# Attention, expert attention and gated mixing on one core: the first batch issued in a written order, its loads reordered, five warming products fewer

## The chip, the core and the metric

The kernel runs on one core of a Trainium2 chip. The core has a matrix engine (PE, with its weight loads shown apart as PEld), a vector engine (DVE), an activation engine (ACT), a general engine (POOL) and a queue engine (SP), which issues nearly all DMAs here; 16 DMA engines move the data. The metric is the device time of one launch in microseconds, lower is better. Three timed runs of the kernel before gave 791.86, 794.79 and 794.84 us; their median, 794.79, is the time to compare with.

## The reference

Three stages in float32 over 8 batches of 576 tokens, each feeding the next:

```python
def _attn_ref(q, k, v, p):            # 8 batches, 8 heads, 576 tokens, 64 wide; p: 32 packed queries
    p_packed = sm_attn(p, k, v)       # softmax(p k^T / 8) v
    return sm_attn(q, p_packed, p_packed)

def _moe_ref(x, w_gate, wq, wk, wv, wo):   # 4 experts of causal attention, 2 of 4 kept per token
    logits = x @ w_gate                    # top 2, softmax over the two
    for e in range(4):
        q, k, v = x @ wq[e], x @ wk[e], x @ wv[e]
        out += weight(e) * (softmax(causal(q @ k.T / 8)) @ v) @ wo[e]

def _moe2_ref(x, mu_k, mu_r, w_k, w_v, w_r):
    xk = mu_k * x + (1 - mu_k) * x_prev    # x_prev: the token before
    xr = mu_r * x + (1 - mu_r) * x_prev
    v = relu(xk @ w_k) ** 2 @ w_v
    return sigmoid(xr @ w_r) * v
```

The weights `w_k`, `w_v` and `w_r` are float64 and are decoded on the chip.

## The kernel before

The work of the first two stages is cut into generators ("steps"): `front` (the first stage of a batch, for each of two groups `g` of four heads), `values`, `project`, `soft`, `turn` and `pair_out` (the second stage), and `fold`, which decodes `w_k` and `w_r` piece by piece and multiplies each by `wo`. Each `yield` of a step has a planned time from a table (`FRONT_T`, `G1_T`, `VAL_T`, `FOLD_0` and the others, in units of which a batch has 20). The program sorts all pieces by these times, issues them in that order, and a scheduler then orders the instructions of each engine by priority and by its own estimate of time. After the last batch come the `r` products, the `k` products and the `v` products of the third stage.

In the code, with the line numbers of the profile: the warming products (16 products of 128x128 on zeros, L168) come first on PE. `front` for one group is: scores `s1` of the packed queries, 8 products 32x288 (`eight`, L220); their maximum `mx` (L268) and `nb` (L270) on DVE; the exponential `a1` on ACT (L273); five transposes on PE (L280) and their copy `aT` on ACT (L205); the product with `v` (L289, 20 pieces); the scaled `pp` on DVE (L296), its transpose (L301) and the copy `ppT` (ACT, L205); the scores `s2` of the 576 tokens (L220 on `qT`); on DVE two transposes `st` (L308), the maximum `m` (L311), the subtraction (L313); the exponential on ACT (L316); the product with the packed input weights `wa` (L220) that is split into `PWh` (ACT, L319) and `PWl` (DVE, L320); the sums `s` (L323), `r` (L327, L328), the multiplication (L329), the transpose `a2` (L332), and its split into `A2h` (ACT, L205) and `A2l` (DVE, L335). The scores `s1`, the transposes, `s2` and the `wa` products share two buffers of PSUM (`big`), `aT` has one buffer.

`values` (L357) and `project` (L412) then take `A2h` and `A2l` of both groups. `project` ends in the casts `qs` and `ks` on ACT (L424, L430), the rest `l` and `kl` on DVE (L425, L431), and four small DMAs that move half a tile (L433, L434); after them the first score products of the second stage can run (L472). One chunk of `decode` is five DVE instructions (`dce` L625, `dcx` L628, `dce` L631, `dcu` L634, `wc` L655), one on ACT (`dcq` L645) and several on POOL; the folding products are L709.

The first loads stand on the SP queue in the order `p k` of both groups, `v q` of group 0, `wo`, two chunks `raw` of `w_k`, `v q` of group 1, the two halves of `wa`; then those of batch 1. For the first batch the small subtractions and multiplications (L313, L329) are on DVE, for the others on POOL. `decode` of the first chunks is held behind instructions of group 0 by `first` and `behind`.

Of the kernel before, what the change touches and what calls it, by code (L numbers as in the profile page):

```python
# [9 lines left out]
F32 = mybir.dt.float32  # L10
# [9 lines left out]
EPS = 1e-9  # L20
# [3 lines left out]
FRONT_T = [-29.98, -26.81, -23.33, -16.88, -17.51, -14.04, -12.67, -12.1, -8.35]  # L24
G1_T = [1.16, 2.59, 3.23, 1.72, 1.63, 8.19, 3.77, 1.61, 3.2]
VAL_T = [-3.35, 0.36, -1.9, 0.35, 0.62]
PROJ_T = [-2.04, -1.82, 1.38, 2.56]
# [4 lines left out]
FOLD_0 = [-21.99, -18.2, -16.87, -12.45, -10.56, -6.17, -3.87, -1.05, -0.52, 1.63, 3.63, 7.17, 8.98]  # L32
FOLD_T = [5.65, 105.86]
WA_AT = -29.61
PR0, WARM = (1000, 946, 1043, 1073, 1037, 1000, 940, 980, 907), 16
WR_AT = 7.41
R_LOAD, R_RUN = ([15.69, 16.11], [22.66, 28.61])
W_AT = [4.54, 4.19]
K_AT = [(0, -1.0, 0)] + [(0, 0.0, j) for j in range(4)] + [(1, -1.0, 0)] + [(1, 0.0, j) for j in range(5)]
E_TURN = "VAAAA"  # L40
E_DIAG = "AAAAV"
E_TURN2 = "AAAAA"
E_DIAG2 = "AAAVA"
E_WH, E_SQ, E_B, E_G, E_CXL = "P", "A", "V", "V", "A"
E_AT, E_VG, E_CB, E_PT, E_PPT, E_CX = "A", "A", "A", "V", "A", "V"
E_Z = "P"
E_DT, E_WL = "P", "P"
PR = {'front': 0, 'values': -100, 'project': 0, 'soft': 0, 'turn': 0, 'out': 236, 'fold': 0, 'k': 46, 'gates': 0}
# [7 lines left out]
def kernel(  # L56
# [83 lines left out]
    if True:  # L140
# [52 lines left out]
        def load_wa():  # L193
            for c in range(0, NG * NH, NH):
                nc.sync.dma_start(wa[:, c : c + NH, :], w_in[:, c : c + NH, :])

# [3 lines left out]
        def pool_copy(o, x):  # L200
            nc.gpsimd.tensor_scalar(o, x, 1.0, 0.0, op0=ALU.mult, op1=ALU.add)

        def evac(eng, o, x):
            if eng == "A":
                return nc.scalar.copy(o, x)  # L205
            if eng == "V":
                return nc.vector.tensor_copy(o, x)
            pool_copy(o, x)
# [4 lines left out]
        def eight(lhs, rhs, n):  # L213
# [3 lines left out]
            for j in range(NH):  # L217
                for hf in range(2):
                    r = slice(64 * hf, 64 * hf + 64)
                    nc.tensor.matmul(  # L220
# [4 lines left out]
                    )  # L225
            return halves(ps)[:, :, :n]

        def load(b, gs):

            for g in gs:  # L230
                pT = pTs[(b * NG + g) % 2]
                nc.sync.dma_start(pT, p[b, g].rearrange("d j n -> d (j n)"))
                kT = ld.tile([P, NH, SH], F32, tag="kT", name=nm("kT"))
                nc.sync.dma_start(kT, k[b, g])
                loaded[b, g] = [pT, kT]
            for g in gs:
                if b == 0 and g == 1:
                    first["won"] = dv.tile([P, NDT, 2 * P], F32, tag="wc", name=nm("won"), bufs=1)
                    nc.sync.dma_start(first["won"], wo.rearrange("(c p) n -> p c n", p=P))
                    first["raw"] = [fetch_raw(w_k, c * P, 0) for c in range(2)]  # L240
                vn = vns[(b * NG + g) % 2]
                nc.sync.dma_start(
                    vn[:, : NT - 1, :], v[b, g, : (NT - 1) * P].rearrange("(c p) x -> p c x", p=P)
                )
                nc.sync.dma_start(vn[TAIL:, NT - 1, :], v[b, g, (NT - 1) * P :])
                qT = ld.tile([P, NH, SH], F32, tag="qT", name=nm("qT"))
                nc.sync.dma_start(qT, q[b, g])
                loaded[b, g] += [vn, qT]

        def mark(b, g, eng, x, ins):  # L250

            if b == 0 and g == 0:
                for turn in {"V": [(0,), (1,), (2, 3)], "A": [(0, 1), (2, 3)]}[eng][x]:
                    first[eng, turn] = ins.ins

        def front(b, g):
# [847 lines left out]
```

## Time and profile before

| what | value |
|---|---|
| timed runs, median | 794.79 us (791.86 to 794.84) |
| profiled execution, whole | 789.45 us |
| profiled execution, first to last instruction | 787.7 us |
| PE busy | 751.6 us, 95% of the span |
| DVE busy | 477.4 us, 61% |
| ACT, POOL busy | 448.7 us, 384.5 us |

The profile comes from one execution. Its stretches differ: the opening (to about 46 us) in which the first batch's `front` has nothing before it to hide behind, the batches (to about 385 us), and the third stage. Shares over the whole span say little on the opening, so the rows below are stretches of it. The granted clock of PE has two levels here, 1.00 (2.4 GHz) and 0.50 (1.2 GHz).

### The profile page before, as it was taken

The numbers are of one execution on the slowest core, as the hardware profiler recorded it, in microseconds if no ns is written. First come the engines' busy times: TensorE is split into PE (matmuls) and PEld (weight loads), VectorE is DVE, ScalarE is ACT, GpSimd is POOL, SyncE is SP. The second block draws the span as 40 slices with busy tenths as digits, with TensorE's granted clock in tenths as the row PEclk, the third lists the DMA queues.
The fourth block names the chain that finished last, engine by engine and source line by source line (L and its number), as shares of the span: only waits on it lengthen the run. The fifth ranks groups of instructions, "written<-read, shape, count | busy, mean of one in ns | idle before, by whom it ended". The sixth has DMA issues, their size and how long they took to land.

```text
span 787.7 us, 15356 instructions
## 1 busy us (share of the span) xinstructions
PE 751.6 (95%) x5504; PEld 617.7 (78%) x5504; DVE 477.4 (61%) x1174; ACT 448.7 (57%) x1029; POOL 384.5 (49%) x484
## 2 busy tenths in 40 slices
PE   6789989999999999998999999999999999999998
PEld 4476968869697887877678888888888888888886
DVE  4979896979868668677767978787581111111111
ACT  2357677678767768786633532422967755555400
POOL 7358776764777635253601533631267443344610
PEclk9599999999999999999999999999999999999999
DMA  9856473655637353315459785867889565555511
GB/s 320 302 151 194 139 226 104 190 151 177 207 105 222 97 166 91 83 43 170 150 201 309 299 296 185 279 196 244 309 286 344 159 187 154 171 177 171 156 67 54
DMA packets 92396, 148.35 MB, mean 188 GB/s; under 512 B 9376, under 2 KB 64160, under 8 KB 90016
## 3 DMA queue, kind: packets, MB, share of 16 engines
q1 hardware_dynamic: 92176, 147.36, 58.7%
q8 instruction: 44, 0.72, 0.4%
q14 instruction: 32, 0.26, 0.1%
q10 hardware_dynamic: 144, 0.00, 0.0%
HBM read 87.04 MB, written 50.33 MB: 174 GB/s over the span
## 4 chain that ended last, share of the span: by engine, by line
PE 74%; DVE 11%; DMA 5%; POOL 4%; ACT 3%; issue 2%; SPq 0%; POOLq 0%; DVEq 0%; ACTq 0%
PE one L929 25%; PE big L888 8%; PE one L888 8%; PE one L557 5%; PE big L412 4%; PE one L868 4%; PE big L868 4%; DMA ms<-ms 4%; PE one L709 3%; PE one L357 3%; PE one L515 2%; PE one L472 2%; DVE ms L490 2%; ACT ms L494 1%; PE big L220 1%
## 5 line engine op out<-in xcount | busy, mean ns | idle before, releaser
L934 DVE TENSOR_TENSOR ring<-one,ring 128x512 f32<-128x512 f32 x36 | 24.9, 692 | 168.3 <-PE one L929 158.8
L929 PE MATMUL one<-wvh,yh 128*128 128x512 f32 x288 | 112.0, 389 | 0.0
L929 PE MATMUL one<-wvl,yh 128*128 128x512 f32 x288 | 112.0, 389 | 0.0
L929 PE MATMUL one<-wvh,yl 128*128 128x512 f32 x288 | 112.0, 389 | 0.0
L494 ACT ACTIVATE ms<-ms,nb 128x192 f32<-128x192 f32 (+3 forms) x128 | 78.4, 616 | 21.3 <-DVE nb L490 21.2
L211 POOL TENSOR_TENSOR yl<-yvh,yh 128x1024 fp32r<-128x1024 f32 (+1 forms) x24 | 49.1, 2060 | 44.7 <-ACT yh L914 24.6
L205 ACT COPY tb<-one 64x128 f32<-64x128 f32 (+5 forms) x208 | 61.4, 362 | 11.3 <-PE one L522 11.2
L640 POOL TENSOR_TENSOR dcx<-dcx,dcu 128x256 f32<-128x256 f32 x40 | 30.7, 768 | 66.1 <-DVE dcu L634 53.5
L929 PEld LDWEIGHTS one<-wvh,yh 128*128 128x128 f32 x288 | 54.1, 188 | 11.3
L929 PEld LDWEIGHTS one<-wvl,yh 128*128 128x128 f32 x288 | 54.1, 188 | 11.3
L929 PEld LDWEIGHTS one<-wvh,yl 128*128 128x128 f32 x288 | 54.1, 188 | 11.1
L211 POOL TENSOR_TENSOR yl<-yvl,yh 128x1024 fp32r<-128x1024 f32 x16 | 38.2, 2396 | 41.0 <-ACT yh L914 19.7
L515 PE MATMUL one<-ident,ms 128*128 128x128 f32 x320 | 53.1, 281 | 3.1 <-ACT ms L494 3.0
L557 PE MATMUL one<-tb,vg 128*64 128x320 f32 (+4 forms) x448 | 53.6, 362 | 0.6 <-DVE nb L490 0.4
L490 DVE CUSTOM_DVE_ANT_0 ms<-one,mstrip 128x192 f32<-128x192 f32 (+2 forms) x96 | 43.5, 481 | 15.9 <-PE one L472 15.2
L557 PEld LDWEIGHTS one<-tb,vg 128*64 128x64 f32 x448 | 33.3, 136 | 18.3 <-issue 1.7
L515 PEld LDWEIGHTS one<-ident,ms 128*128 128x128 f32 x320 | 36.2, 141 | 13.5 <-ACT ms L494 8.3
L211 POOL TENSOR_TENSOR dt<-cb 128x192 f32<-128x192 f32 (+1 forms) x48 | 31.4, 684 | 30.9 <-DVE cb L575 24.2
L1051 ACT ACTIVATE ring<-ring 128x1024 f32<-128x1024 f32 x18 | 19.0, 1059 | 34.9 <-DMA ring<-rscr 34.9
L472 PE MATMUL one<-ks,qs 128*128 128x192 f32 (+3 forms) x128 | 36.6, 300 | 0.4 <-ACT vg L205 0.3
L522 PE MATMUL one<-ident,ms 128*128 128x128 f32 x96 | 27.4, 287 | 9.3 <-DMA ms<-ms 8.7
L661 POOL TENSOR_TENSOR wl<-wc,wh 128x256 fp32r<-128x256 f32 x48 | 34.9, 751 | 0.3
(208 smaller groups left out, 2071.1 us busy)
## 6 DMA issues: line engine op xcount, KB each, us to landing
yscr<-y SPq DMA_DIRECT2D x48, 384.0 KB, 3.5
dl<-dscr SPq DMA_DIRECT2D x40, 256.0 KB, 5.8
yvh<-yscr SPq DMA_DIRECT2D x10, 1024.0 KB, 5.9
kT<-in_k_dram SPq DMA_DIRECT2D x16, 576.0 KB, 4.2
qT<-in_q_dram SPq DMA_DIRECT2D x16, 576.0 KB, 5.7
rscr<-rr SPq DMA_DIRECT2D x12, 768.0 KB, 4.4
ring<-rscr SPq DMA_DIRECT2D x36, 256.0 KB, 2.9
out_dram<-ring SPq DMA_DIRECT2D x36, 256.0 KB, 3.2
```

The costliest lines, as they stand in the source:

```text
L205: return nc.scalar.copy(o, x)
L211: nc.gpsimd.tensor_tensor(o, x, y, op=op)
L412: nc.tensor.matmul(ps[:, 512 * hf : 512 * hf + SH], ww[:, g, :], xx[:, g, :], start=i == 0, stop=i == 3 * NG - 1,)
L472: nc.tensor.matmul(ps[:, po : po + kn], qs[:, qo : qo + P], keys[:, ko : ko + kn], start=x == 0, stop=x == 1,)
L490: nc.vector.tensor_tensor_reduce(halves(mv) if last else mv, sv, halves(mk) if last else mk, op0=ALU.add, op1=ALU.min, scale=-SC, scalar=3 ...
L494: nc.scalar.activation(to, mv, AF.Exp, bias=nb[:n], scale=-1.0, accum_out=bat["sums"][:n, i, e : e + 1],)
L515: nc.tensor.transpose(ps[:, at + j * P : at + (j + 1) * P], ms[:, j * P : (j + 1) * P], ident)
L557: nc.tensor.matmul(av[64 * ee : 64 * ee + 64, qo - lo : hi - lo], vg[:, j, HD * (2 * ep + ee) : HD * (2 * ep + ee + 1)], tslice(tabs[ee], ...
L661: nc.gpsimd.tensor_sub(l, x, f32(h))
L868: nc.tensor.matmul(po, dx[:, NS * t + s, t0 : t0 + P], wpart("r", s, wx, t), start=n == 0, stop=n == 3 * KT - 1,)
L888: nc.tensor.matmul(po.rearrange("p (b n) -> p b n", b=2), wpart("k0" if f < 4 else "k1", s, wx, t)[:, f % 4 * P : f % 4 * P + P], dx[:, :, ...
L929: nc.tensor.matmul(ps, a[:, f, P * t : P * t + P], wres["v"][b][:, f, :], start=n == 0, stop=n == 3 * NFT - 1,)
```

## The change

For batch 0 every product of PE and the instructions of DVE and ACT that lie on the way of `front` are issued in the order in which the steps are given (`seq`, which ties each to the one before it on its engine). That order comes from new tables of step times, one for each group (`OPEN_T0`, `OPEN_T1`); batch 0 no longer uses `FRONT_T`. The decoding of the first piece is tied behind later instructions than before (`TIES_V`, `TIES_A`). The loads of the first batch are listed by name in `LOADS`. The warming products go from 16 to 11, and `fill` puts seven small products (128x64) on zeros behind some steps of the first batch. The other tables of times and priorities have new values, and the copy of the last diagonal block of a head (`E_DIAG[4]`, 64x64) goes from DVE to ACT in batches 0 to 3. What is computed stays the same.

```diff
-FRONT_T = [-29.98, -26.81, -23.33, -16.88, -17.51, -14.04, -12.67, -12.1, -8.35]
+FRONT_T = [-30.06, -26.81, -23.33, -16.88, -17.51, -14.67, -12.67, -12.1, -8.35]
+OPEN_T0 = [-30.95, -26.9, -23.4, -18.5, -18.46, -16.91, -15.8, -12.55, -12.53]
+OPEN_T1 = [-29.74, -25.62, -23.14, -17.97, -18.04, -18.19, -15.74, -12.38, -12.36]
...
+LOADS = 'k0 k1 v0 v1 q1 q0 wo wa r r'
+TIES_V, TIES_A = [5, 3, 5, 5], [5, 4, 5, 5]
+FILL = [[0, 4, 0, 0, 1, 0], [0, 2, 0, 0, 0, 0]]
+SEQ = 'VTA'
-PR0, WARM = (1000, 946, 1043, 1073, 1037, 1000, 940, 980, 907), 16
+PR0, WARM = (1050, 946, 1080, 1073, 1037, 896, 869, 980, 1107), 11
...
-E_DIAG = "AAAAV"
+E_DIAG = 'AAAAA'
...
+        def seq(b, eng, make):
+
+            with behind(chain.get(eng) if b == 0 and eng in SEQ else None):
+                ins = make()
+            if b == 0:
+                chain[eng] = ins.ins
+            return ins
...
+        def fill(b, g, x, ps, o, ins):
+
+
+            for _ in range(0 if b else FILL[g][x]):
+                with tc.issue_after(ins.ins):
+                    nc.tensor.matmul(
+                        ps[:, o : o + 64], mstrip[:, :P], mstrip[:, P : P + 64], start=True, stop=True
+                    )
...
-            s2 = eight(ppT, qT, SH)
+            s2 = eight(b, g, 4, ppT, qT, SH)
             st = fr.tile([P, S], F32, tag="sa", name=nm("st"), bufs=4)
             for hf in range(2):
-                nc.vector.transpose(st[:, SH * hf : SH * hf + SH], s2[:, hf, :])
+                seq(b, "V", lambda: nc.vector.transpose(st[:, SH * hf : SH * hf + SH], s2[:, hf, :]))
```

On the SP queue, the loads of the first batch stand in this order before (`vn_126`, `vn_127`: `v` of groups 0 and 1; `qT_167`, `qT_177`: `q` of groups 0 and 1; two earlier `pT` and `kT` pairs stand ahead of them in both):

```order
L242 DMA vn_126<-in_v_dram 128x4x256
L245 DMA vn_126<-in_v_dram 64x256
L247 DMA qT_167<-in_q_dram 128x1152
L239 DMA won_169<-in_wo_dram 128x4x256
L775 DMA raw_171<-in_w_k_dram 128x512
L775 DMA raw_173<-in_w_k_dram 128x512
L242 DMA vn_127<-in_v_dram 128x4x256
L245 DMA vn_127<-in_v_dram 64x256
L247 DMA qT_177<-in_q_dram 128x1152
L195 DMA wa<-in_w_in_dram 128x1544 x2
```

And now (`qT_164` is group 1's, `qT_166` group 0's):

```order
L259 DMA vn_126<-in_v_dram 128x4x256
L262 DMA vn_126<-in_v_dram 64x256
L259 DMA vn_127<-in_v_dram 128x4x256
L262 DMA vn_127<-in_v_dram 64x256
L267 DMA qT_164<-in_q_dram 128x1152
L267 DMA qT_166<-in_q_dram 128x1152
L280 DMA won_168<-in_wo_dram 128x4x256
L277 DMA wa<-in_w_in_dram 128x1544 x2
L835 DMA raw_172<-in_w_k_dram 128x512
L835 DMA raw_174<-in_w_k_dram 128x512
```

Both `v` and both `q` have moved ahead of `wo` and of the chunks of `w_k`, and `wa` ahead of those chunks.

On DVE, from the second group's `pp` on, before (`raw_171` and `raw_173` are chunks of `w_k`, `big_299` and `big_361` the scores `s2` of groups 0 and 1):

```order
L296 TENSOR_SCALAR pp_293<-one_272,ri_22_217 128x128
L655 SCALAR_TENSOR_TENSOR wc_326<-dcq_332,dcx_329 128x256
L308 STREAM_TRANSPOSE st_308<-big_299 128x288 x2
L311 TENSOR_REDUCE m_37_311<-st_308 128x18
L313 TENSOR_TENSOR st_308<-st_308,m_37_311 128x576
L625 TENSOR_SCALAR dce_349<-raw_173 128x256
L628 SCALAR_TENSOR_TENSOR dcx_348<-raw_173,dce_349 128x256
L631 TENSOR_SCALAR dce_349<-dcx_348 128x256
L323 TENSOR_REDUCE s_46_342<-st_308 128x9x2
L634 SCALAR_TENSOR_TENSOR dcu_350<-raw_173,dce_349 128x256
L327 TENSOR_SCALAR r_47_344<-s_46_342 128x18
L320 TENSOR_TENSOR PWl_158<-big_315,PWh_157 128x772
```

And now from the same place (`big_296` is `s2` of group 1, `big_312` of group 0):

```order
L349 TENSOR_SCALAR pp_290<-one_269,ri_22_212 128x128
L362 STREAM_TRANSPOSE st_305<-big_296 128x288 x2
L365 TENSOR_REDUCE m_37_308<-st_305 128x18
L368 TENSOR_TENSOR st_305<-st_305,m_37_308 128x576
L362 STREAM_TRANSPOSE st_322<-big_312 128x288 x2
L365 TENSOR_REDUCE m_40_325<-st_322 128x18
L368 TENSOR_TENSOR st_322<-st_322,m_40_325 128x576
L378 TENSOR_REDUCE s_43_355<-st_322 128x9x2
L375 TENSOR_TENSOR PWl_153<-big_333,PWh_152 128x772
L382 TENSOR_SCALAR r_44_357<-s_43_355 128x18
L385 RECIPROCAL r_44_357<-r_44_357 128x18
L386 TENSOR_TENSOR st_322<-st_322,r_44_357 128x576
```

The decoding has left this place; group 1 is taken first, then group 0 is carried through, and the sums of group 0 follow its subtraction at once.

On PE, what stands around the first score products of the second stage; before, just ahead of them and behind them (`one_682`, `one_694`: scores; `PWh`, `A2l`: the last values; all 24 folding products of the first slot, L709, stand further ahead):

```order
L357 MATMUL one_617<-PWh_157,A2l 128x260
L472 MATMUL one_682<-ks_556,qs_112 128x192
L472 MATMUL one_682<-kl_114,qs_112 128x192
L472 MATMUL one_682<-ks_556,qs_112 128x320
L472 MATMUL one_682<-kl_114,qs_112 128x320
L412 MATMUL big_649<-A2h,PWh_157 128x288 x2
```

And now, further behind them (`one_696`: the next scores; `one_565`, `one_580`: the folding products, of which 6 of 24 stand ahead of `one_684`, the first scores):

```order
L531 MATMUL one_696<-ks_550,qs_112 128x64
L531 MATMUL one_696<-kl_114,qs_112 128x64
L769 MATMUL one_565<-wh_366,woTh 128x256
L769 MATMUL one_565<-wl_367,woTh 128x256 x3
L769 MATMUL one_580<-wh_366,woTh 128x256
L769 MATMUL one_580<-wl_367,woTh 128x256 x3
L769 MATMUL one_565<-wl_367,woTh 128x256
L769 MATMUL one_565<-wh_366,woTl 128x256 x4
```

Eighteen folding products have gone from ahead of the first scores to behind the second ones.

## Rows read from the trace of the kernel before

**Rows 1.** The page: busy time by engine.

```profile
PE 751.6 (95%) x5504; PEld 617.7 (78%) x5504; DVE 477.4 (61%) x1174; ACT 448.7 (57%) x1029; POOL 384.5 (49%) x484
```

**Rows 2.** Stretches: us; PE, PEld, DVE, ACT, POOL busy (instructions); clock; DMA.

```profile
18.00:20.00 2.00, 0.15 (x8) 0.18 (x16) 1.85 (x4) 0.66 (x2) 1.27 (x4) 0.50 1.00 395
...
38.00:40.00 2.00, 2.00 (x16) 2.00 (x15) 1.51 (x4) 1.10 (x3) 1.37 (x3) 0.93 0.50 122
46.07:67.00 20.93, 16.42 (x204) 13.35 (x205) 18.83 (x60) 12.67 (x38) 12.60 (x19) 1.00 0.61 179
```

**Rows 3.** Timeline, 0 to 20 us: start, us, engine, line, what [idle before <-releaser].

```profile
1.62 6.67 PE L168 MATMUL one<-mstrip 128*128 128x128 f32 x32 [1.62 <-DVE lower L113]
...
8.22 1.20 PE L220 MATMUL big<-kT,pT 64*32 64x288 f32 x32
...
12.14 0.76 PE L280 MATMUL big<-ident,a 128*128 128x128 f32 x5 [0.34 <-ACT a L273]
...
13.72 0.69 ACT L205 COPY aT<-big 128x640 f32<-128x640 f32 x1 [1.05 <-PE one L289]
...
16.25 0.77 PE L289 MATMUL one<-vn,aT 128*32 128x64 f32 x40 [1.85 <-DMA vn<-in_v_dram]
...
16.95 0.71 PE L220 MATMUL big<-qT,ppT 64*32 64x288 f32 x16
...
17.96 0.27 ACT L205 COPY ppT<-one 128x128 f32<-128x128 f32 x1 [2.92 <-PE one L301]
...
18.45 0.84 DVE L308 STREAM_TRANSPOSE st<-big 128x288 f32<-128x288 f32 x2
...
19.85 1.54 PE L220 MATMUL big<-wa,ppT 64*32 64x386 f32 x16 [1.93 <-DMA wa<-in_w_in_dram]
```

**Rows 4.** Timeline, 20 to 36 us.

```profile
20.12 0.91 DVE L313 TENSOR_TENSOR st<-st,m 128x576 f32<-128x576 f32 x1
...
21.93 0.75 DVE L323 TENSOR_REDUCE s<-st 128x18 f32<-128x576 f32 x1
...
25.93 1.22 PE L220 MATMUL big<-kT,pT 64*32 64x288 f32 x16 [0.38 <-PE big L220]
...
32.44 1.33 PE L280 MATMUL big<-ident,a 128*128 128x128 f32 x5 [1.71 <-ACT a L273]
32.75 0.77 DVE L332 STREAM_TRANSPOSE a<-st 128x576 f32<-128x576 f32 x1
...
34.28 0.58 PE L357 MATMUL one<-PWh,A2h 128*128 128x260 f32 x1 [0.51 <-ACT A2h L205]
```

**Rows 5.** Stretches with five decoding instructions, and one with the maximum `mx`.

```profile
20.95:21.93 0.98, 0.98 (x24) 0.25 (x8) 0.91 (x4) 0.87 (x2) 0.00 (x0) 0.50 1.06 395
22.59:22.93 0.34, 0.00 (x0) 0.00 (x0) 0.34 (x3) 0.00 (x0) 0.00 (x0) 0.50 1.00 374
24.05:24.33 0.28, 0.28 (x8) 0.19 (x16) 0.28 (x3) 0.00 (x0) 0.00 (x0) 0.50 1.10 360
30.23:30.90 0.67, 0.50 (x11) 0.00 (x0) 0.67 (x3) 0.00 (x0) 0.00 (x0) 0.50 1.05 398
```

**Rows 6.** Timeline, 39 to 47 us.

```profile
39.24 0.64 ACT L424 CAST qs<-big 128x576 fp32r<-128x576 f32 x1
...
40.98 0.64 ACT L430 CAST ks<-big 64x576 fp32r<-64x576 f32 x1 [0.56 <-PE big L412]
41.05 0.74 DVE L425 TENSOR_TENSOR l<-big,qs 128x576 fp32r<-128x576 f32 x1
...
43.08 0.56 SPq L433 DMA_DIRECT2D ks<-ks  x1
...
46.07 0.33 PE L472 MATMUL one<-ks,qs 128*128 128x192 f32 x1 [0.28 <-ACT vg L205]
```

**Rows 7.** The chain of waits, 0 to 70 us: start, us, what (the folding products).

```profile
40.95 2.14 PE one L709 x18
```

**Rows 8.** PE's waits from 380 us to the end: total, times, longest, us.

```profile
PE one L522 <- DMA ms<-ms: 0.3, 1, 0.3
```

More of the change, by code (lines that the diff above doesn't have):

```diff
@@ L224, in eight, with load_k @@
                         start=True, stop=True,
-                    )
+                    ))
+            fill(b, g, x, ps, 448, ins)
             return halves(ps)[:, :, :n]
[L228 to L237, printed above, removed]
+        def load_k(b, g):
+            pT = pTs[(b * NG + g) % 2]
+            nc.sync.dma_start(pT, p[b, g].rearrange("d j n -> d (j n)"))
+            kT = ld.tile([P, NH, SH], F32, tag="kT", name=nm("kT"))
+            nc.sync.dma_start(kT, k[b, g])
+            return pT, kT
@@ new lines, in load_v, with load_q, load_first @@
+        def load_v(b, g):
+            vn = vns[(b * NG + g) % 2]
+            nc.sync.dma_start(
+                vn[:, : NT - 1, :], v[b, g, : (NT - 1) * P].rearrange("(c p) x -> p c x", p=P)
+            )
+            nc.sync.dma_start(vn[TAIL:, NT - 1, :], v[b, g, (NT - 1) * P :])
+            return vn
+        def load_q(b, g):
+            qT = ld.tile([P, NH, SH], F32, tag="qT", name=nm("qT"))
+            nc.sync.dma_start(qT, q[b, g])
+            return qT
+        def load_first():
+            got = {}
+            first["raw"] = []
+            for x in LOADS.split():
+                if x == "wa":
+                    for c in range(0, NG * NH, NH):
+                        nc.sync.dma_start(wa[:, c : c + NH, :], w_in[:, c : c + NH, :])
+                elif x == "wo":
@@ L606, in fetch_raw @@
             return raw
-        def behind(ins):
-            return tc.issue_after(ins) if ins is not None else nullcontext()
         def decode(dst, src, r0, f0, raw=None, turn=None):
@@ L623, in decode @@
             }
-            with behind(first["V", turn] if turn is not None else None):
+            with behind(tie("V", turn and TIES_V[turn - 1])):
                 nc.vector.tensor_scalar(
@@ L643, in decode @@
             if E_SQ == "A":
-                with behind(first["A", turn] if turn is not None else None):
+                with behind(tie("A", turn and TIES_A[turn - 1])):
                     nc.scalar.activation(f32(t["q"]), f32(hi), AF.Square)
@@ L970 @@
                 add(
-                    "front", front(b, g), [t0 + t + g * G1_T[i] for i, t in enumerate(FRONT_T)],
-                    None if b else [x - 10 * g for x in PR0],
+                    "front", front(b, g),
+                    [t0 + t + g * G1_T[i] + (LATE1[g] if b == 1 and not i else 0.0) for i, t in enumerate(FRONT_T)]
+                    if b else (OPEN_T0, OPEN_T1)[g],
+                    None if b else list((PR0, PR1)[g]),
                 )
```

153 lines of the change are left out of this document (85 added, 68 removed).

## The prediction

> **What bounds the kernel now.** I read the page's busy times, then stretches of the opening with the granted clock, the timeline from 0 to 47 us, the chain of waits, and last PE's waits in the third stage. PE is the fullest engine, 95% of the span [rows 1], so a microsecond is saved for good only where PE waits, or where it runs at 1.2 GHz. Both happen at the start. The clock is at 0.50 by 18 us, with PE busy 0.15 of 2 us, and comes back between 38 and 40 us, where PE is busy without a gap [rows 2]. PE's dense work starts at 34.28 us, when `A2h` of group 1 is there [rows 4], so about 4.0 us of it run at half speed.
>
> What holds that start back is read in three places. Sixteen warming products run from 1.62 to 8.29, and the first scores begin at 8.22 though nothing but the warming stands ahead of them [rows 3]. Group 1's product with `v` starts at 16.25, ended by its load, and `wa` at 19.85, ended by its load [rows 3]. And DVE, from the first `st` at 18.45 to the end of the last `a2` at 33.52 [rows 3, 4], runs almost without a pause, with decoding between the steps of the batch; that is 15.07 us. From 46.07 to 67 DVE is the fuller engine, 18.83 of 20.93 us against PE's 16.42 [rows 2].
>
> **The change part by part.**
>
> *Warming.* One product takes 6.67 / 16 = 0.417 us; five fewer are 2.08. The first scores then begin at 6.21. Before, both groups' scores took 1.20 us after the warming; at half clock one group takes 1.22 [rows 3, 4]. I take the half clock for them, since PE will have run two microseconds less: group 0 ends at 7.43, where before it ended at 8.82. The lead is 1.4 us; at full clock it would be 2.0.
>
> *Loads.* 1600 KB (by their shapes 512 for `wo`, 256 for each of two chunks, 576 for `q` of group 0) leave the way of group 1's `v`. At 395 GB/s [rows 2] that is 4.1 us, so it lands at about 12.1 instead of 16.2; the two `q` follow, 1.5 us each, at 13.6 and 15.1. `wa` passes two chunks, 512 KB or 1.3 us: the first half at 18.5, the second some 2 us later.
>
> *PE up to `s2`.* Group 1's transposes move from 12.14 to 10.74 and end at 11.5. The fill products have no row. A 128-column product at half clock takes 0.417, so one of 64 columns takes 0.1 (full clock) to 0.21; the two behind these transposes end at 11.7. The four behind group 0's fall into a gap of 0.34 us [rows 3] and cost 0 to 0.5; I take 0, since at 0.1 each they nearly fit. Group 0's `v` product runs to 12.5. `aT` has one buffer, its second copy waited for that product before too [rows 3], so it runs to 13.25; between them `pp` and its transpose fit. Group 1's `v` product, whose load is there, runs from 13.3 to 14.07. From there to the end of `ppT` took 18.23 - 17.02 = 1.21 us [rows 3]: 15.28. `s2` of group 1 takes 0.71 and DVE starts 0.2 later: the first `st` at 16.2 instead of 18.45.
>
> *DVE from there to `a2` of group 1.* Between the two places stood nine decoding instructions, now four. The five that leave (`dce`, `dcx`, `dce`, `dcu`, `wc`) took 0.98 + 0.34 + 0.28 = 1.60 us [rows 5]. One maximum of batch 1 comes in, 0.67 [rows 5]. And a stall opens: the sums follow the subtraction at once, and from its end, 21.03, to the sums at 21.93 are 0.90 us [rows 4] that the decoding filled before. Together 15.07 - 1.60 + 0.67 + 0.90 = 15.04, so `a2` ends at 31.25, 2.3 us earlier, and PE turns dense at 32.0 instead of 34.28. `wa` is hidden behind the subtractions, which end at about 21.
>
> *To the first scores.* Eight `values` products, two folding products and twelve `project` products follow, the same as before. If the clock rises 4.0 us after the start again, `qs` is cast by 39.88 - 2.3 = 37.6. Before, `l` began only at 41.05, behind decoding; now it stands ahead of the last chunks and starts at 37.6. `ks` is cast by 41.62 - 2.3 = 39.3 and its DMA no longer waits behind the others, so it goes at 39.35 instead of 43.08; the scores began 2.99 us after it [rows 6]: 42.3 instead of 46.07, a lead of 3.75 us. Part of that is borrowed: 18 folding products, 2.14 us of PE [rows 7], now come later, so PE itself leads by 1.6.
>
> *Behind them.* From 46.07 to 67 PE idles 20.93 - 16.42 = 4.5 us, more than the 2.14 borrowed, while DVE idles 2.1 [rows 2]. With DVE ahead by the whole lead, most of the debt should fit into PE's gaps; they are not where the products now stand, so I count a quarter of it, 0.55, as lost. The gain is 3.75 - 0.55 = 3.2 us, between 1.6 (nothing fits) and 3.75.
>
> *The rest.* Sixteen small copies go from DVE to ACT, spread over four batches; neither engine is full there, 0 within 0.5 either way. At the start of the third stage 16 `r` products of 0.23 us move ahead of the last batch's last products, 3.6 us at most if the later loads then come late; but PE waits only 0.3 us in all after 380 [rows 8], so I take 0. The other step times hardly move.
>
> *The sum.* 787.7 - 3.2 + 1.75 around the span = 786.25 for an execution like the profiled one (789.45). That one lies 5.34 under the median of the timed runs, so the prediction is 794.79 - 3.2 = 791.6.
>
> **Rivals.** About 0.5% (4.0 us) is what a measurement here tells from no change.
>
> (a) The debt does not fit: DVE, 90% busy in that stretch, is no faster for the lead, and the 18 products stand in front of batch 1's product with `v`. Gain 1.6: 793.2. For it speaks that PE's gaps there are ended by other engines; against it that DVE's work is the same and starts earlier.
>
> (b) The debt fits and the clock comes back as soon as PE is dense, or never falls. Then the 4.0 us at half speed become 2.0: gain 3.75 + 2.0 = 5.75, and if PE's other gaps of that stretch shrink by the lead, 7: 789.0 to 787.8. For it the fill products and a denser PE up to 16 us; against it that PE has little to do from 17 to 31 us in both kernels.
>
> (c) Slower: the shorter warming does not bring the clock up, and PE runs at 1.2 GHz from the start to the dense stretch. On the way lie group 1's transposes (1.33 for 0.76 [rows 3, 4]: 0.57), two `v` products (0.77 more each, if half the clock doubles them), and `s2` (about 0.5): 2.6 us. The first `st` is then at 18.8, `a2` and the first scores 0.3 later than before, and the 2.14 of moved products come on top: 2.4 slower, 797.2; with the clock back one microsecond later than after 4.0, another 0.5. It decides if the granted clock is 0.50 between 8 and 16 us. Against it: PE has work without a gap to 8.65 us even so, because the slower scores fill the place. The Trainium skill ("TensorE: Matmul & The Clock Gate", "What's actually happening") says that the low clock is the default and that activity releases it, which speaks for (c), since activity is what the change takes away; by it the time would be that of (c). The trace agrees that the warming ran at the low clock: 0.417 us a product.
>
> (d) The change may not do what it says where a load sets the pace: if `v` of group 1 lands as late as before, 16.2, the gain shrinks to (a). The DMA engines are full in that stretch, 1.00 [rows 2], so the order of issue should be the order of landing.
>
> **How the numbers follow.** Forecast 0.50 (its own range 789.5 to 793.2), (a) with (d) 0.22, (b) 0.15, (c) 0.13. The forecast is faster by over 4.0 us in four tenths of its cases (0.20), (b) in nearly all (0.14), (a) hardly (0.02): 0.36. (c) is slower by over 4.0 in half of its cases and (a) rarely: 0.07. The rest, 0.57, is within. The range leaves out the ends of (b) and (c): 787.8 to 796.5.
>
> **What would show it.** First scores at about 6.2 us; group 1's `v` product at 13.3 with no wait for its load; the first `st` at 16.2; `A2h` of group 1 by 32.0; the first scores of the second stage at 42.3; PE's idle time in the 21 us behind them under 3 us. I am wrong if the clock is low before 16 us, if DVE stalls for more than the 0.9 us named, or if the lead at 42 us is gone by 70.

## The result and the profile after

The changed kernel took 797.36 us (median of seven timed runs; 795.1 to 800.5) against 794.28 us for the kernel before on the same chip. One more execution of the changed kernel took 2000.67 us and is left out here. The ratio on record is 1.0061, 95% interval 1.0035 to 1.0086; the two medians alone give 1.0039. So it is slower by 0.4 to 0.6%, where 0.4% faster was forecast. On a second chip (e13 below) the ratio was 1.0040, interval 1.0009 to 1.0071. The profiled execution took 796.97 us, its span 795.2.

The opening went almost as forecast. The timeline of PE (start, duration, instruction, then the idle time just before it and what ended it), to be read against [rows 3, 4]:

```profile
1.62 5.06 PE L177 MATMUL one<-mstrip 128*128 128x128 f32 x22 [1.62 <-DVE lower L122]
6.61 1.32 PE L241 MATMUL big<-kT,pT 64*32 64x288 f32 x32
...
13.69 0.77 PE L341 MATMUL one<-vn,aT 128*32 128x64 f32 x40
...
15.61 1.21 PE L241 MATMUL big<-qT,ppT 64*32 64x288 f32 x32 [0.35 <-ACT ppT L210]
...
18.39 0.88 PE L241 MATMUL big<-wa,ppT 64*32 64x386 f32 x16 [1.21 <-DMA wa<-in_w_in_dram]
20.36 1.40 PE L241 MATMUL big<-wa,ppT 64*32 64x386 f32 x16 [1.08 <-DMA wa<-in_w_in_dram]
...
30.70 1.33 PE L331 MATMUL big<-ident,a 128*128 128x128 f32 x5 [1.85 <-ACT a L324]
32.82 0.58 PE L416 MATMUL one<-PWh,A2h 128*128 128x260 f32 x1 [0.78 <-ACT A2h L210]
```

First scores at 6.61 (forecast 6.2: the five products fewer saved 6.67 - 5.06 = 1.61 us and not 2.08), the second `v` product at 13.69 with no wait for a load (13.3), dense work from 32.82 (32.0; before 34.28). From there the forecast goes astray. DVE between 36 and 40 us, then the DMA of `ks` and PE's first scores of the second stage:

```profile
36.39 0.29 DVE L685 TENSOR_SCALAR dce<-raw 128x256 int32<-128x256 int32 x1 [0.85 <-DMA raw<-in_w_k_dram]
36.60 0.42 DVE L715 SCALAR_TENSOR_TENSOR wc<-dcq,dcx 128x256 f32<-128x256 f32 x1
37.05 0.42 DVE L688 SCALAR_TENSOR_TENSOR dcx<-raw,dce 128x256 int32<-128x256 int32 x1
37.51 0.38 DVE L691 TENSOR_SCALAR dce<-dcx 128x256 int32<-128x256 int32 x1
37.92 0.92 DVE L694 SCALAR_TENSOR_TENSOR dcu<-raw,dce 128x256 f32<-128x256 uint32 x1
38.88 0.46 DVE L685 TENSOR_SCALAR dce<-raw 128x256 int32<-128x256 int32 x1
39.26 0.74 DVE L484 TENSOR_TENSOR l<-big,qs 128x576 fp32r<-128x576 f32 x1
```

```profile
41.53 0.55 SPq L492 DMA_DIRECT2D ks<-ks  x1
...
44.10 0.33 PE L531 MATMUL one<-ks,qs 128*128 128x192 f32 x1 [1.08 <-DMA ks<-ks]
```

`l` stands behind the third chunk's decoding and the first instruction of the fourth, and starts at 39.26 instead of the forecast 37.6; the first scores come at 44.10, a lead of 1.97 us over [rows 6] and not 3.75. Twenty microseconds later PE waits 2.80 us (the kernel before waits 1.48 at about the same place). Behind `ms` (L553) stands DVE, and behind DVE a chunk of `w_k` still in flight. PE in the changed kernel and in the kernel before, DVE's waits from 45 to 80 us in the changed kernel (total, times, longest), then the SP queue's issues, the last line that of the kernel before:

```profile
66.53 0.33 PE L578 MATMUL one<-ident,ms 128*128 128x128 f32 x1 [2.80 <-ACT ms L553]
```

```profile
66.78 0.55 PE L515 MATMUL one<-ident,ms 128*128 128x128 f32 x3 [1.48 <-ACT ms L494]
```

```profile
DVE dce L685 <- DMA raw<-in_w_k_dram: 3.1, 1, 3.1
```

```profile
54.23 0.46 SPq L492 DMA_DIRECT2D ks<-ks  x1
56.85 0.39 SPq L259 DMA_DIRECT2D vn<-in_v_dram  x1
57.33 0.47 SPq L493 DMA_DIRECT2D ks<-ks  x1
57.92 0.50 SPq L835 DMA_DIRECT2D raw<-in_w_k_dram  x1
```

```profile
52.02 0.55 SPq L775 DMA_DIRECT2D raw<-in_w_k_dram  x1
```

That is the eighth chunk. It was issued at 52.02 in the kernel before and is issued at 57.92 now, behind a `v` load that had to wait for its buffer; DVE wants it at 61.4 and has it at 64.55.

Whether PE gained anything is seen by what it had done. Stretches from 0 to 45 and 45 to 90 us (length, busy time and instructions of PE, PEld, DVE, ACT, POOL, granted clock, DMA share, GB/s), of the kernel before, then of the changed one:

```profile
0.00:45.00 45.00, 32.18 (x335) 24.21 (x336) 31.57 (x78) 16.53 (x33) 27.23 (x58) 0.77 0.86 291
45.00:90.00 45.00, 40.08 (x431) 32.48 (x430) 37.67 (x119) 30.00 (x89) 33.03 (x52) 1.00 0.54 158
```

```profile
0.00:45.00 45.00, 30.48 (x333) 23.20 (x334) 30.77 (x77) 16.54 (x34) 23.23 (x50) 0.81 0.84 282
45.00:90.00 45.00, 40.63 (x421) 32.75 (x420) 36.77 (x112) 29.37 (x89) 35.26 (x55) 0.96 0.53 166
```

By 45 us DVE has done 77 instructions against 78, and POOL is 4.0 us behind. Of PE's products 32 were warming before, and now 22 are warming and 14 fill, so it has done 297 of the kernel's own against 303. The opening was put in another order; no work was taken out of it. Without warming and fill (6.67 us before, 5.06 + 1.00 + 0.56 + 0.43 now) PE's busy time is 25.5 and 23.4 us, 2.1 less; the clock gives back at most 1.7 of it, with 17.1 instead of 20.5 us at 1.2 GHz.

### The profile page after: what moved, and what is told of

The parts are those of the page before. It is cut to its first block, busy times and chain, and to the rows that moved or that the text cites. A ratio compares the mean times of both kernels' runs of the same rounds, so it can differ in the third digit from the quotient of the medians.

```text
span 795.2 us, 15361 instructions
## 1 busy us (share of the span) xinstructions
PE 756.0 (95%) x5508; PEld 621.3 (78%) x5508; DVE 482.8 (61%) x1158; ACT 450.1 (57%) x1045; POOL 385.1 (48%) x484
## 4 chain that ended last, share of the span: by engine, by line
PE 73%; DVE 12%; DMA 8%; ACT 4%; POOL 2%; issue 2%; SPq 0%; DVEq 0%; POOLq 0%; ACTq 0%
PE one L989 25%; PE one L948 8%; PE big L948 8%; PE big L471 4%; PE one L928 4%; PE big L928 4%; PE one L620 4%; DMA ms<-ms 3%; PE one L769 3%; PE one L416 3%; PE one L531 2%; PE one L578 2%; DMA raw<-in_w_k_dram 2%; DVE ms L549 2%; ACT ms L553 1%
## 5 line engine op out<-in xcount | busy, mean ns | idle before, releaser
L553 ACT ACTIVATE ms<-ms,nb 128x192 f32<-128x192 f32 (+3 forms) x128 | 78.5, 617 | 25.0 <-DVE nb L549 25.0
L210 ACT COPY tb<-one 64x128 f32<-64x128 f32 (+5 forms) x224 | 64.3, 351 | 12.6 <-PE one L585 12.5
L989 PEld LDWEIGHTS one<-wvh,yl 128*128 128x128 f32 x288 | 54.1, 188 | 11.3
L531 PE MATMUL one<-kl,qs 128*128 128x192 f32 (+3 forms) x128 | 36.1, 315 | 0.0
```

The source lines that it names most:

```text
L531: nc.tensor.matmul(ps[:, po : po + kn], qs[:, qo : qo + P], keys[:, ko : ko + kn], start=x == 0, stop=x == 1,)
L553: nc.scalar.activation(to, mv, AF.Exp, bias=nb[:n], scale=-1.0, accum_out=bat["sums"][:n, i, e : e + 1],)
L989: nc.tensor.matmul(ps, a[:, f, P * t : P * t + P], wres["v"][b][:, f, :], start=n == 0, stop=n == 3 * NFT - 1,)
```

## The experiments

The theory was a *decoding debt*: the decoding of the first chunks is put off, its first instruction by 12.5 us (13.94 us before, 26.43 now), and what was put off is paid behind 45 us. In the trace of the changed kernel the first chunk still runs mostly ahead of the last transpose of the batch's second softmax (`dce` at 26.43, the transpose at 31.29); the second to fourth chunk follow it. Rivals: the shorter warming and the clock; the new step times; and, from the second group of runs on, a *fitted order* (any edit makes a new order of everything behind it, and the order of the kernel before fits better than a new one).

Ratios are against the kernel before on the same chip, with 95% intervals.

**e13 and e12: both kernels a second time.**

> The changed kernel as it is, on the chip of the next three. Theory (decoding debt): PE's wait behind the ms of L553 at 66 us and DVE's wait for a chunk at 61 us are there again within 0.3 us, since they come from the order; the falls of the clock stand elsewhere, or are fewer or more. Time 3 to 5 us over the kernel before.

> The kernel before as it is, for a second profile on the chip of these runs. The first one was 789.45 us, 5.3 under the median, and its clock never fell between 38 and 787 us. The theory that falls of the clock come to both kernels alike (so that they do not explain the difference of the medians): this one shows 1 to 4 falls of 3 to 7 us between 45 and 400 us, each behind an idle time of PE of over 1 us, at 791 to 796 us.

PE's wait at 66 us came again, 2.81 us at 66.03, as did DVE's, 3.0 us; the time was 2.6 us over the kernel before, a little under the forecast. The second profile of the kernel before took 797.54 us, 8.1 more than the first, on the same instructions: up to 300 us it is 0.9 us behind the first, with a fall of 3.4 us at 68.1, and then the clock is at 0.50 twice for 6.8 us, from 303.6 behind a wait of 3.09 us and from 375.3 behind one of 2.88. The first profile has waits of 1.82 and 2.29 at these two places and no fall. The mean time at 1.2 GHz per run was 24.6 us in the changed kernel and 30.9 in the kernel before (e13's timed runs, from the clock of each): falls of the clock come to both, and do not explain the difference. Not all of them are chance, though: the changed kernel's falls at 68 and 259 us, 3.4 us each, stand in both of its profiles, and the one at 259 in neither profile of the kernel before.

From here on profiles are compared by PE's *place*: the products it has started by a time, each counted with the median time of the products on the same tiles in the kernel before, without warming and fill products; microseconds behind that kernel's first profile (worked out from the traces; minus is ahead):

| | 45 | 60 | 70 | 90 | 120 | 200 | 300 | ratio |
|---|---|---|---|---|---|---|---|---|
| before, second profile | -0.4 | 0.0 | 0.4 | 1.2 | 0.6 | 0.6 | 0.9 | |
| changed | 0.6 | 0.3 | 0.9 | 2.1 | 2.5 | 1.3 | 4.2 | 1.0061 |
| changed, second (e13) | 0.2 | -0.2 | 0.6 | 1.9 | 2.0 | 1.1 | 3.3 | 1.0040 (1.0009 to 1.0071) |
| e2 before, late decoding | 0.7 | 2.2 | 0.2 | 3.5 | 3.4 | 5.3 | 4.0 | 1.0081 (1.0056 to 1.0106) |
| e3 changed, old step times | 0.6 | 0.3 | -0.6 | 1.7 | 3.5 | 4.4 | 3.6 | 1.0083 (1.0055 to 1.0112) |
| e4 changed, chunks by ACT | 1.0 | 0.6 | -1.2 | -0.6 | 1.6 | 4.1 | 4.6 | 1.0078 (1.0054 to 1.0101) |
| e5 before, 11 products | 3.3 | 1.7 | 1.5 | 3.3 | 4.0 | 6.4 | 4.9 | 1.0050 (1.0029 to 1.0072) |
| e7 before, no decoding | -0.6 | -0.8 | -1.8 | -2.3 | 0.6 | 3.5 | 4.9 | 1.0001 (0.9977 to 1.0025) |
| e8 changed, no decoding | -1.0 | -0.8 | -0.9 | -1.5 | 1.0 | 0.0 | 1.6 | 0.9999 (0.9975 to 1.0022) |
| e14 before, new step times | 0.7 | 0.2 | 0.6 | 2.2 | 2.6 | 2.5 | 2.4 | 1.0069 (1.0040 to 1.0097) |

Two profiles of the changed kernel agree within 0.5 us up to 200 us, those of the kernel before within 1.2; a smaller difference says nothing. The two of the changed kernel lose another 2 to 3 us between 200 and 300, where the second of the kernel before loses 0.3.

**e2: the kernel before, with only the decoding put off.** It puts off more than the change does: here the first chunk starts behind the last transpose too, at 32.72 us instead of 26.43, and the eighth is issued at 62.18 instead of 57.92:

```diff
-FOLD_0 = [-21.99, -18.2, -16.87, -12.45, -10.56, -6.17, -3.87, ...
+FOLD_0 = [-21.99, -18.2, -16.87, -5.1, -5.0, -4.5, -3.87, ...
...
-            with behind(first["V", turn] if turn is not None else None):
+            with behind(first["V", [5, 3, 5, 5][turn - 1]] if turn else None):
```

> The kernel before with one thing moved: the first four chunks are decoded behind the last transpose of group 1's second softmax on DVE, as in the changed kernel. Warming, loads, step times of all else stay. Theory (decoding debt): the chunks are loaded late as in the changed kernel, DVE stalls 1 to 4 us on one of them between 50 and 75 us, and the lead at the first scores of the second stage does not last: slower than before by 2 to 5 us, 796.5 to 799. Rivals (warming and clock, step times): nothing of what they blame is in here, so DVE is only freed in the opening and the time is 791 to 794.5.

Slower by 0.8%, as the theory wants; the chunks from the third on are issued 10 to 15 us later than before, and the lead at the first scores (43.85 us, 2.2 ahead) is lost by 60 us. DVE's stall was not on a chunk here, though, and the dose is larger than the change's.

**e7 and e8: both kernels without that decoding.** In each, one copy stands for a chunk's seven instructions, so these kernels leave out the decoding of the first four chunks; in e8 the second chunk's copy is also tied behind the last transpose:

```diff
+            if turn is not None:
+                with behind(...):
+                    nc.vector.tensor_scalar(dst, f32(hi), 0.015625, None, op0=ALU.mult)
+                return
```

> The kernel before without the decoding of the first four chunks: one DVE copy of the raw words stands for each chunk's five DVE, one ACT and one POOL instructions, so the weights are not the right ones. It takes 16 DVE instructions (some 8 us) out of the first 40 us. It is there to be compared with the next run. By itself: 1 to 4 us faster than before, since DVE has no decoding between the steps of the first batch.

> The changed kernel with the same left out (one DVE copy for each of the first four chunks, the weights not the right ones; the copies stand behind the last transpose). Theory (decoding debt): without the postponed work the opening's lead lasts, so this is no slower than the same cut in the kernel before: within 1.5 us of it or faster. Rivals (brittle schedule, warming, step times): it stays slower than that one by 3 us or more, as the changed kernel is slower than the kernel before.

Of e7, then of e8, 0 to 90 us:

```profile
0.00:45.00 45.00, 32.68 (x340) 24.32 (x340) 25.35 (x64) 16.13 (x32) 25.14 (x57) 0.77 0.86 287
45.00:90.00 45.00, 41.19 (x444) 34.63 (x445) 37.33 (x123) 31.71 (x93) 31.29 (x49) 1.00 0.58 173
```

```profile
0.00:45.00 45.00, 31.74 (x347) 23.91 (x348) 25.93 (x62) 15.33 (x31) 25.61 (x57) 0.85 0.84 289
45.00:90.00 45.00, 41.33 (x436) 33.61 (x436) 39.49 (x118) 31.93 (x96) 32.03 (x49) 0.96 0.54 165
```

The two are equal, as the theory says: without this decoding the changed opening costs nothing. It also brings nothing. The contrast is weak, though: the interval of e8 overlaps that of the changed kernel's second measurement (1.0009 to 1.0071). And with 5 to 6 us of DVE less by 45 us, PE has done 784 - 32 = 752 and 783 - 36 = 747 of the kernel's products by 90 us, where with the decoding in place it had done 734 and 718 (the windows above): a lead of 1.5 to 2.3 us that neither time shows. e7's forecast of 1 to 4 us faster failed. A lead at 90 us is not a lead at the end.

**e4: the stall at 61 us taken away.** Chunks from the third on are loaded from ACT's queue, past the waiting `v` load:

```diff
-            dma = nc.sync.dma_start(dst, src)
+            dma = (nc.sync if late or "go" not in first else nc.scalar).dma_start(dst, src)
```

> The changed kernel with the chunks from the third on loaded from ACT's queue instead of SP's, so that none stands behind a load that waits for its buffer. In the changed kernel the eighth chunk's buffer is free at 55.9 us, but its load is issued at 57.92, behind a v load that waits until 56.85. If the queue on SP makes the stall: the eighth chunk is issued by 56.2, DVE's wait for it falls from 3.1 to under 1.5 us, time 795 to 797. If the late decoding alone makes it: the wait stays over 2 us, time 797 to 799. ACT may lose up to 0.5 us where it waits for a buffer itself.

The chunk was issued at 56.9 us and DVE no longer waits long for one; PE's longest wait from 45 to 80 us is now 0.9. But the time did not fall. PE's waits from 80 to 180 us in e4:

```profile
PE one L586 <- DMA ms<-ms: 3.6, 2, 2.2
PE big L472 <- DVE nb L550: 3.1, 2, 2.8
```

PE leads by 1.2 us at 70 us and is 1.6 behind at 120. A wait of 2.8 has gone at 66 us and one of 2.8 has come at 99. So the visible stall is real and is not the price.

**e1 and e6: decoding put back between the steps.** e1 gives the changed kernel the old ties and the old order of loads; e6 loads two chunks behind the `v` loads and decodes them in DVE's gaps:

```diff
# e1
-LOADS = 'k0 k1 v0 v1 q1 q0 wo wa r r'
+LOADS = 'k0 k1 v0 q0 wo r r v1 q1 wa'
-TIES_V, TIES_A = [5, 3, 5, 5], [5, 4, 5, 5]
+TIES_V, TIES_A = [0, 1, 2, 2], [0, 0, 1, 1]
# e6
+LOADS = 'k0 k1 v0 v1 r r q1 q0 wo wa'
+TIES_V, TIES_A = [0, 4, 2, 2], [0, 3, 4, 4]
```

> The changed kernel, but the first four chunks of the decoding stand between the steps of the first batch again (each tied to the step that it was tied to before) and the first loads are in the order of before, since the two chunks must be there early. The written order of the batch's own steps, the eleven warming products, the fill products and the new step times stay. Theory (decoding debt): the 14 us by which the first decoding instruction starts later is never made up, every later chunk is loaded 6 to 12 us later than before, DVE runs into a chunk that is still in flight at 61.4 us and stalls 3.1 us, and PE behind it 2.8. Then here: no DVE wait of over 1 us on a chunk between 50 and 80 us, no PE idle time of over 2 us and no clock at 0.50 there, time 793 to 795.5. Rival (warming and clock): the loss comes from the shorter warming, then about 798 stays. Rival (step times): the new tables cost all through the first 400 us, then about 798 stays too.

> The changed kernel with the first two chunks loaded right behind the v loads and decoded in the gaps that DVE has there (the first behind pp of the first group done, the others between the steps of the second softmax), instead of behind the last transpose. In the changed kernel DVE is idle for 4.7 of the 8 us ahead of its first st at 16.43, and POOL from 20.4 to 30.8. Theory (decoding debt): the chunks' loads stand 1 to 5 us from those of the kernel before instead of 6 to 12, the opening loses at most 2 us, and the lag against the kernel before no longer rises between 50 and 115 us; time 790 to 794. Rivals (brittle schedule, warming, step times): 796 to 800.

Both were slower still: e1 1.0105 (1.0076 to 1.0134), e6 1.0129 (1.0092 to 1.0167). Neither tests the debt, since each lost the opening first: PE is 4.5 and 5.5 us behind at 45 us. In e6 the product with `wa` waits on DVE, which stands in front of the first chunk's `wc` until POOL is done (DVE, then PE):

```profile
22.50 0.43 DVE L715 SCALAR_TENSOR_TENSOR wc<-dcq,dcx 128x256 f32<-128x256 f32 x1 [8.01 <-POOL dcx L700]
```

```profile
23.79 1.54 PE L241 MATMUL big<-wa,ppT 64*32 64x386 f32 x16 [6.51 <-DVE st L362]
```

**e15: part of the decoding on ACT and POOL.** For the first four chunks `dcu` goes to ACT and POOL, the last product to POOL:

```diff
-            if E_B == "V":
+            if E_B == "V" and not turn:
-            if E_G == "P":
+            if E_G == "P" or turn:
```

> The changed kernel with two of the five DVE instructions of each of the first four chunks on ACT and POOL instead (0.42 to 0.9 us each in the changed kernel, 8 of them, some 4.5 us of DVE); the same values. POOL is idle from 20.4 to 30.8 us there. Theory (decoding debt): the dense stretch starts up to 1 us earlier, the chunks' loads come 1 to 3 us earlier, the time lies between the changed kernel and the one with no decoding of these chunks: 1 to 3 us faster than the changed kernel. If the debt sits in POOL's part of the chain rather than in DVE's: no gain, or slower.

1.0261 (1.0236 to 1.0286), far outside the forecast. The moved ACT instruction waits 7.13 us for its chunk in front of `ppT`, and PE for `ppT`:

```profile
21.06 0.43 ACT L698 ACTIVATE dcu<-raw 128x256 f32<-128x256 uint32 x1 [7.13 <-DMA raw<-in_w_k_dram]
```

```profile
21.70 2.17 PE L241 MATMUL big<-qT,ppT 64*32 64x288 f32 x32 [6.44 <-ACT ppT L210]
```

It shows what a chunk's load costs when it stands in front of the batch's own step, and says nothing on the dose.

**e3 and e14: the step times.** e3 is the changed kernel with the old `FRONT_T`, `G1_T`, `VAL_T`, `PROJ_T`, `FOLD_0`, `FOLD_T`, `W_AT`, `R_LOAD`, `R_RUN`, `PR` and diagonal copies (and `WR_AT` and `LATE1`); e14 the kernel before with the new ones, of which two lines:

```diff
# e14
-PR = {'front': 0, 'values': -100, 'project': 0, 'soft': 0, 'turn': 0, 'out': 236, 'fold': 0, 'k': 46, 'gates': 0}
+PR = {'front': 0, 'values': -100, 'project': 0, 'soft': 0, 'turn': 0, 'out': 178, 'fold': 0, 'k': 33, 'gates': 0}
...
```

> The changed kernel with the step times, priorities and copy engines outside the opening as before (fronts of later batches, values, project, folding, third stage, the diagonal copies); the opening's own times, order, loads, fill products and late decoding stay. Theory (decoding debt): the stall on a chunk between 55 and 70 us is still there, time 797 to 799. Rival (step times): 793 to 795, and the lag behind the kernel before does not grow after 80 us.

> The kernel before with the changed kernel's step times, priorities and copy engines outside the opening (fronts of later batches, values, project, folding, third stage, the diagonal copies); the opening, its decoding, loads and warming as before. Theory (decoding debt) alone: within 1.5 us of the kernel before. Rival (the order behind the opening was fitted to the old opening and every new one is worse): 2 to 5 us slower, with PE within 1 us of the kernel before up to 60 us.

Either mixture is slower than the kernel before by 0.7 to 0.8%. e14 decodes early, opens like the kernel before and is within 0.2 us of it at 60 us; it loses later. That is the fitted order, and a rival that the debt theory has to share the loss with. It also takes weight from e2: an edit with no debt costs nearly as much, and the debt theory alone had forecast under 1.5 us for e14.

The two runs also tell one cost of the new step times from the rest. PE's waits from 200 to 300 us, in the changed kernel, then in e14:

```profile
PE big L241 <- DVE kl L490: 1.6, 1, 1.6
```

```profile
PE big L220 <- DVE kl L431: 1.6, 1, 1.6
```

The wait ends at 204 us in both profiles of the changed kernel and at 206 in e14, where PE idles 4.35 us in this stretch, against 2.77 and 3.11 in the two profiles of the kernel before (by place e14 loses nothing there). A wait behind `kl` (0.9 to 1.6 us) stands between 200 and 300 us in nine of the ten profiles of kernels with the new step times (not in e4), and in none of the eight with the old ones, e3 among them. It goes with the step times, whatever the opening does. Yet e3 is no faster: it has lost 4.4 us by 200 us.

**e5, e9, e10, e11: warming and fill products.** e5 is the kernel before with `WARM` 11, e9 the changed kernel with 16. e10 and e11 put fill products into PE's gaps:

```diff
# e10, changed kernel
-FILL = [[0, 4, 0, 0, 1, 0], [0, 2, 0, 0, 0, 0]]
+FILL = [[0, 4, 0, 0, 5, 8], [0, 2, 0, 0, 0, 4], [5, 0, 0, 0, 0, 0], [5, 0, 0, 0, 0, 0]]
# e11, kernel before
+        FILL = {(0, 0): [0, 5, 4], (0, 1): [0, 5, 8], (1, 0): [5, 0, 0], (1, 1): [5, 0, 0]}
```

> The kernel before with 11 warming products instead of 16 and nothing else. Decoding stands where it stood. Theory (decoding debt): nothing of the loss is in the warming; within 0.5% of the kernel before, 0 to 2 us faster or slower. Rival (warming and clock): slower by 2 us or more, with more time at 1.2 GHz in the first 40 us than the 20.5 of before. Rival (brittle schedule: any shift at the start upsets an order that was fitted to the old one, and every variant loses 4 to 6 us): slower by 4 us or more.

> The changed kernel with sixteen warming products again instead of eleven, nothing else. Five products fewer cost the kernel before 4 us. If the changed kernel's loss is partly the shorter warming: 1 to 4 us faster than the changed kernel, 793.5 to 796 where the kernel before takes 792.6, with less time at 1.2 GHz in the first 45 us. If it is the postponed decoding alone: the opening is 0 to 1 us later and the time is as the changed kernel's or 1 us over it, 796.5 to 799.

> The changed kernel with fill products (64 columns, 0.25 us each by the trace of the changed kernel) in PE's gaps between 17 and 31 us: 4 more behind the first batch's second scores, 8 and 4 behind the two products with wa, 5 behind each of batch 1's first scores. PE idles 8 us there in gaps of 0.8 to 2.2 us. If the granted clock falls at 20.6 us for want of work on PE: it stays at 1.00 through 38 us, the dense stretch loses 2 us, time 794 to 796.5; if the decoding debt then still sets the pace: 796 to 798. If the clock falls all the same and the products stand in the way: 798 to 801.

> The kernel before with such fill products: 5 behind each of the first batch's second scores, 4 and 8 behind the products with wa, 5 behind each of batch 1's first scores; nothing else. If the clock stays at 1.00 through the opening (it was 20.5 us at 0.50): 1.5 to 3 us faster than before, 789.5 to 791. If the clock falls all the same: 792 to 795.

e5 1.0050, as the warming rival said, where the debt theory had at most 2 us (27.3 us at 1.2 GHz in its profile's opening against 20.5, and PE 3.3 us behind at 45). But e9, with the products back in the changed kernel, was worse: 1.0132 (1.0111 to 1.0152), although its opening had only 13.7 us at 1.2 GHz and PE was 1.6 us behind at 45 us; it was 5.4 behind at 120 and 8.6 at 200. So neither count is better by itself; what e9 lost behind 45 us is of the fitted order's kind, and e5's loss is as large as that rival asked for too. e10 1.0108 (1.0089 to 1.0128): the clock fell at 25.0 us instead of 20.6, came back at 42.1 instead of 37.7, and PE was 5.3 us behind at 45. e11 1.0139 (1.0119 to 1.0158): 1.2 GHz from 11.3 to 42.0 us, PE 8.1 behind. The fill products did not hold the clock.

**e16: the DMA of the `ms` corner replaced by a POOL copy,** in the kernel before:

```diff
-                    nc.sync.dma_start(ms[:64, 2 * P : 2 * P + 64], first_[64:, P : P + 64])
+                    pool_copy(ms[:64, 2 * P : 2 * P + 64], first_[64:, P : P + 64])
```

> The kernel before with the corner of ms (64x64) copied by POOL instead of by a DMA, nothing else. PE waits 8.7 us for these DMAs between 44 and 400 us. If these waits bound the time: 3 to 7 us faster. If POOL, 0.6 to 0.9 busy there, brings the copy no sooner than the DMA's 1.7 us: within 2 us of before, or slower.

1.0080 (1.0056 to 1.0103), slower. Once more the order behind it changed with it, so the run does not tell what the waits for these DMAs alone are worth.

Over all runs the debt theory's forecasts of the time came true in e2, e3 and e8, and failed in e1, e5, e6, e14 and e15, of which e1, e6 and e15 had spoilt the opening first.

## Why the prediction was wrong

*Right.* Warming, loads, PE up to `s2` and the start of the dense stretch came within 0.8 us. Rival (c) did not happen in the changed kernel: the clock was at 1.00 from 6.9 to 20.6 us. Rival (d) did not either: no wait for `v`.

*The step that failed first: "To the first scores".* It put `l` at 37.6, ahead of the last chunks. DVE was at 36.39 still in the third chunk, waiting for its load, and `l` started at 39.26; `ks` was issued at 41.53 instead of 39.35, and the lead of 3.75 us was 1.97. The step ahead of it, "DVE from there to `a2` of group 1", had prepared this. It counted the five decoding instructions that leave that stretch rightly, but the stretch took 15.63 us (16.43 to 32.06) and not 15.04, and the five had only moved to where `l` stands: DVE did 77 instructions for 78 by 45 us.

*The debt of 18 products.* The prediction took 2.14 us of it off the lead and expected PE to be 1.6 us ahead. With a lead of 1.97 nothing is left (1.97 - 2.14 = -0.17): PE's place at 45 us is 0.6 and 0.2 behind in the two profiles. There was no gain to carry on. Rival (a), at 793.2, rested on the same lead and fell with it.

*PE's gaps behind the first scores.* Forecast: under 3 us idle in 21. Measured, 20.90 - 18.83:

```profile
44.10:65.00 20.90, 18.83 (x233) 15.77 (x233) 15.93 (x50) 11.09 (x31) 15.13 (x25) 1.00 0.61 183
```

2.1 us, so this was right, but part of the 2.80 us wait lies beyond it. PE fills its gaps with the 18 late products, and the wait for the late chunk comes behind them.

*The step that failed for the sign: "The rest", where "the other step times hardly move" stood for 0.* A gain of nothing gives 794.3; by the medians 3.1 us more were measured, and 2.6 on the second chip. Where PE loses them is read from its idle time by stretch (45 to 200 and 200 to 300 us; columns as above), of the kernel before, its second profile, the changed kernel and its second profile:

```profile
45.00:200.00 155.00, 144.83 (x1543) 119.32 (x1541) 129.13 (x406) 108.24 (x318) 104.46 (x168) 1.00 0.57 168
200.00:300.00 100.00, 97.23 (x1107) 79.88 (x1105) 72.89 (x235) 71.59 (x217) 62.45 (x103) 1.00 0.55 163
```

```profile
45.00:200.00 155.00, 145.53 (x1534) 119.29 (x1534) 127.79 (x405) 108.26 (x318) 103.97 (x166) 0.99 0.57 167
200.00:300.00 100.00, 96.89 (x1108) 79.38 (x1102) 72.16 (x232) 70.43 (x212) 62.99 (x104) 1.00 0.54 162
```

```profile
45.00:200.00 155.00, 145.59 (x1535) 120.32 (x1536) 129.16 (x394) 108.28 (x329) 108.52 (x175) 0.99 0.56 169
200.00:300.00 100.00, 94.05 (x1060) 77.46 (x1057) 68.70 (x216) 66.83 (x202) 61.41 (x101) 0.98 0.50 150
```

```profile
45.00:200.00 155.00, 145.12 (x1534) 119.82 (x1534) 128.59 (x392) 107.82 (x328) 108.14 (x174) 0.99 0.57 168
200.00:300.00 100.00, 94.66 (x1065) 78.06 (x1062) 69.20 (x217) 67.50 (x205) 61.83 (x103) 0.98 0.52 151
```

From 45 to 200 us PE idles 9.4 and 9.9 us in the changed kernel, 10.2 and 9.5 before: no more. The chunk's stall at 66 us (2.80 against 1.48) is in there and is made up. From 200 to 300 it idles 5.95 and 5.34 us against 2.77 and 3.11, about 2.7 more, and 1.6 of that is the wait behind `kl` that goes with the new step times (e3 and e14). There too the clock falls for 3.4 us at 259, which costs at most 1.7 us. So what can be placed of the loss lies over 150 us behind the opening, and the term put at nothing has a part in it. This is not the whole account, since with the old step times (e3) the loss stands ahead of 200 us instead.

*The postponed decoding.* Its price is not measured. e8 against the changed kernel, 0.4 to 0.6%, would hold the whole loss, but e8 leaves the decoding's work out rather than moving it back, its order is a new one too, and e7 shows that leaving it out gains nothing in the kernel before. e2 puts off more than the change does, and e14 and e16 show that an order without any debt can lose as much.

*What stays open.* How the 3 us divide between the postponed decoding and an order that fits less well was not settled: every edit here also made a new order behind it, and of the variants none was faster than the kernel before. No run held the later order fixed while the opening changed, and none had the written order or the new order of loads alone. The rival that ended on the right side, (c), was right about a number (797.2) by luck and wrong about the mechanism.

## What to carry to other kernels

When steps of one kind move ahead on a full engine, list what they overtake and follow it to where it is done: work moved on the engine that bounds the next stretch is not a gain there, whatever the first milestone shows. Measure a lead by the work that the bounding engine has done, not by when its next stage starts. Add up its idle time stretch by stretch before blaming the longest wait in sight: here a stall of 2.80 us was made up within 130 us, and the loss stood elsewhere. In a kernel whose order is made by a scheduler from fitted numbers, an edit in one place is also a change of everything behind it, and e14 puts that at as much as the edit itself; compare each edit with another that moves the order but should do nothing.

## What the runs showed of the hardware

A busy PE in the records did not mean full clock here. In e11, with fill products in every gap, from 16 to 40 us (columns as above):

```profile
16.00:30.00 14.00, 13.75 (x135) 8.79 (x136) 7.76 (x18) 2.09 (x4) 4.51 (x9) 0.50 1.05 373
30.00:40.00 10.00, 10.00 (x69) 7.93 (x68) 6.54 (x14) 3.21 (x6) 2.15 (x2) 0.50 0.46 144
```

The granted clock stayed at 0.50, 1.2 GHz, from 11.3 to 42.0 us with PE busy 23.75 of 24 us in these two stretches. The Trainium skill ("TensorE: Matmul & The Clock Gate", "What's actually happening") says that activity releases the throttle; this trace shows that activity as the records count it did not.

After a dense stretch has begun, the clock came back 4.0 us later before, 4.8 in the changed kernel, PE busy throughout in both; in e5 PE was busy 6.64 of the 7.63 us before it came back at 42.1. After waits of 2 to 3 us in the middle of the kernel it fell or did not: 2.29 us at 368 us had no fall in the first profile of before, 2.23 us at 257 had one of 3.4 us in the changed kernel, 3.09 us at 301 one of 6.8 in the second profile of before. On identical instructions the second profile of before was at 1.2 GHz for 17.1 us between 45 and 790, which costs at most 8.5, and the first not at all; the two lay 8.1 us apart.
